# Stores of zeros issued twice, once more before the last part's loads of a decode-attention kernel

## The chip, the cores and the metric

The kernel runs on one core of a Trainium2 chip. The metric is device time in microseconds (us): the median of several runs of the whole program. Engines: TensorE (PE) does matmuls, VectorE (DVE), ScalarE (ACT) and GpSimd (POOL) do element work, and SyncE (SP) only issues transfers. Transfers run on 16 DMA engines; each engine of the core works through its own instructions in order.

## The reference

Two attention blocks decode one token and are mixed by a gate. Block A has 16 query heads with their own keys and values, block B 16 query heads on 8 key/value heads; each has 8192 cached positions of width 256, all in float32.

```python
def attend(x, k_cache, v_cache, wq, wo):                       # A: 16 kv heads, B: 8 (each serves two queries)
    q = (x @ wq).reshape(B, 1, 16, 256).transpose(0, 2, 1, 3)
    scores = jnp.einsum("bhqd,bhkd->bhqk", q, k) * (256 ** -0.5)
    o = jnp.einsum("bhqk,bhkd->bhqd", softmax(scores, axis=-1), v)
    return o.transpose(0, 2, 1, 3).reshape(B, 1, 16 * 256) @ wo

g = sigmoid((x * gate_w).sum(-1, keepdims=True))               # x: 1 x 1 x 448
out = g * attend(x, A...) + (1 - g) * attend(x, B...)          # 1 x 1 x 448
```

## The kernel before

All inputs but one weight lie in one array, `stream`, in the order of use. The kernel reads it once, front to back, through a ring of three large buffers, `slot_0` to `slot_2` (`SLOTS = 3`, each 128 partitions x 15872 floats, 8.1 MB). The list `LOADS`, made by `plan()`, has 54 entries; entry `number` fills the slot `number % 3`. Most entries are one transfer; the entry before last consists of three (the rest of one tile of values, and two whole tiles), and the last one, "the last part", of nine: the last tile of values in three pieces, three pieces of the output projection's weights, and three pieces of halves of the same weights. All these loads are issued by SP, on line 198 as every instruction that goes through the recorder.

The loop at the end of `build` sets the order of everything. For each entry it issues the entry's loads, and behind each load `piece` writes out the work on what it holds. Keys (`"k"`) become scores: for two of three heads on PE with a row of VectorE, ScalarE and VectorE work behind it (tiles `sc`, `mn`, `st`, `px`, `pr`), for the third, the heads `BY_ROW`, on VectorE, which multiplies the slot in place by the query (`slot<-slot,qa`) and reduces it (`sr<-slot`), 128 x 4096 numbers each time. Values (`"v"`) are multiplied by the weights `pr` on PE into `o`. When a head's keys are done, `gather` and `combine` (tiles `gs`, `mnr`, `ew`, `es`, `z`, `rz`, `wr`) make the softmax's sums; when its values are done, `take` copies `o` out (`px<-ps_o`, `ob`), `project_o` and `emit` apply the output weights. `wait` and `tick` put `combine` and `column` (tile `sel`) off by one or two tiles.

A recorder (`Recorder.call`) adds the semaphore waits: an instruction waits for what it depends on, through SBUF and PSUM, and on each engine the order is the order of the calls. A load into a slot waits until the work on the slot's earlier contents is done; a store waits until its source is written.

The result is one row of 448 numbers, held as four rows of 112 in the tile `ys`, and leaves in two stores, `store(0)` on ScalarE's queue and `store(1)` on SP's. At the end of the kernel each half is copied from PSUM into `ys` and stored. Before that the same two stores are issued once with zeros: `ys` is zeroed by VectorE among the constants, and the two stores stand in front of entry 3, the first that reuses a slot.

Of the kernel before, what the change touches and what calls it, by code (L numbers as in the profile page):

```python
# [28 lines left out]
SLOTS = 3  # L29
# [25 lines left out]
def plan():  # L55

    size = {"xg": XG, "k": ROWS * DH, "v": ROWS * DH, "wq": WQ, "wo": 8 * D}
    per = len(UNITS) * NT
    n = len(TILES)
    items = []  # L60
    for i in range(n + LEAD):
        if i == 0:
            items += [("xg", 0), ("wq", 0)]
        if i < n:
            items.append(("k", i))
        if i >= LEAD:
            items.append(("v", i - LEAD))
        if i % per == 7 and i // per + 1 < NS:
            items.append(("wq", i // per + 1))
        if i % per == LEAD + 1 and i >= per:  # L70
            items.append(("wo", i // per - 1))
    loads, room = [[]], FULL
    last = [("v", n - 3), ("v", n - 2)]
    for kind, i in items[:items.index(last[0])]:
        at, left = 0, size[kind]
        if (kind, i) == ("wq", DS):
            at, left = KF * 2 * DH, left - KF * 2 * DH
        while left:
            step = min(left, room) // ATOM[kind] * ATOM[kind]
            if step:  # L80
                loads[-1].append((kind, i, at, step))
            at, left, room = at + step, left - step, room - step
            if left:
                loads.append([])
                room = FULL

    loads = [[x] for x in loads]
    x = loads[-2][0]
    loads[-2] = [x[:2], x[2:]]
    loads[-1] += [[(kind, i, 0, size[kind])] for kind, i in last]  # L90
    at, end = 0, []
    for c in LAST_CUT:
        end.append([("v", n - 1, at, c * DH)])
        at += c * DH

    for h, n in ((0, 2), (1, 2), (3, 2)):
        end.append([("wo", NS - 1, 2 * h * D, n * D)])
    end += [[("half", 0, 0, D)], [("half", 1, 0, D // 2)], [("half", 1, D // 2, D // 2)]]
    return loads + [end]


LOADS = plan()
# [137 lines left out]
def program(nc, stream, dealt, out):  # L240
    nc.alloc_sbuf_tensor("pad", [P, -((nc.sbuf_base + 31) // 32 * 32) % 256 // 4 or 64], F32)
    memory = {("slot", i): nc.alloc_sbuf_tensor(f"slot_{i}", [P, FULL], F32) for i in range(SLOTS)}
    plan = Recorder(nc, memory)
    build(plan, stream, dealt, out)
    names = ["tensor", "vector", "scalar", "gpsimd"] + plan.dmas
    sems = {n: nc.alloc_semaphore(f"{n[0]}{n[1]}" if n[0] == "dma" else n) for n in names}
    rec = Recorder(nc, memory, plan.needed | {(e, plan.count[e] - 1) for e in names[:4]}, sems)
    stores = build(rec, stream, dealt, out)
    late = rec.wait("sync", [(e, rec.count[e] - 1) for e in names[:4]] + [d for d in rec.dmas if d not in stores[1:]])
    for sem, value in late:  # L250
        nc.sync.wait_ge(sem, value)
    nc.sync.sem_clear(range(sems[names[0]].num, sems[stores[1]].num))
    for d in stores[1:]:
        nc.sync.wait_ge(sems[d], 16)
    nc.sync.sem_clear(range(sems[stores[1]].num, sems[stores[-1]].num + 1))


def build(nc, stream, dealt, out):
# [323 lines left out]
        STORES.append(store(c))  # L582

    ys = const.tile([P, YN], F32, name="ys")
    nc.vector.memset(ys, 0.0)

    def store(c):

        to = out.rearrange("a b (g n) -> (a b g) n", g=NG)[2 * c:2 * c + 2, :]
        return (nc.scalar, nc.sync)[c].dma_start(to, ys[64 * c:64 * (c + 1)][::32, :])  # L590
# [67 lines left out]

    off = 0
    for number, fill in enumerate(LOADS):  # L660
        if number == SLOTS:
            store(0)
            store(1)
        buf = ring.tile([P, FULL], F32, name="slot")
        c = 0
        for load in fill:
            n = sum(x[3] for x in load)
            nc.sync.dma_start(buf[:, c:c + n], stream[off:off + P * n].rearrange("(p n) -> p n", p=P))
            off += P * n
            for x in load:  # L670
                piece(*x[:3], buf[:, c:c + x[3]])
                c += x[3]
# [79 lines left out]
```

## Time and profile before

| | |
|---|---|
| median of 3 runs | 1005.48 us (1005.34 to 1005.86) |
| profiled execution | 1005.52 us, span of its instructions 1004.2 us |
| PE busy | 584.8 us (58%) |
| DVE busy | 461.5 us (46%) |
| ACT busy | 94.1 us (9%) |
| POOL busy | 6.1 us (1%) |
| bytes moved by DMA | 432.49 MB, mean 431 GB/s |

The span runs from the first to the last instruction; the 1.3 us by which the execution is longer lie around it. Times in rows count from the span's start. A row of the profile's timeline gives start, length, engine, line, operation, output <- inputs, shapes and count, then in brackets how long the engine had been idle and what ended that. `SPq` and `ACTq` are the queues of SP and ScalarE as they issue transfers. The page's slices cut the span into 40 pieces of 25.1 us each.

### The profile page before, as it was taken

The numbers are of one execution on the slowest core, as the hardware profiler recorded it, in microseconds if no ns is written. First come the engines' busy times: TensorE is split into PE (matmuls) and PEld (weight loads), VectorE is DVE, ScalarE is ACT, GpSimd is POOL, SyncE is SP. The second block draws the span as 40 slices with busy tenths as digits, with TensorE's granted clock in tenths as the row PEclk, the third lists the DMA queues.
The fourth block names the chain that finished last, engine by engine and source line by source line (L and its number), as shares of the span: only waits on it lengthen the run. The fifth ranks groups of instructions, "written<-read, shape, count | busy, mean of one in ns | idle before, by whom it ended". The sixth has DMA issues, their size and how long they took to land.

```text
span 1004.2 us, 7432 instructions
## 1 busy us (share of the span) xinstructions
PE 584.8 (58%) x3162; PEld 171.7 (17%) x3162; DVE 461.5 (46%) x646; ACT 94.1 (9%) x308; POOL 6.1 (1%) x12
## 2 busy tenths in 40 slices
PE   1755755665753674646645565764655637636567
PEld 0211211121210221112111121111211112101112
DVE  3297222962249521486215851248521585215851
ACT  0100110001100110001100010100110000110011
POOL 2000000000000000000000000000000000000000
PEclk9877687678777887777777867777887777777888
DMA  9999999999999999999999999999999999999998
GB/s 395 442 438 432 426 436 444 422 433 438 443 428 422 441 443 427 420 445 438 428 430 438 435 428 440 430 431 435 433 443 422 431 443 433 431 427 443 435 414 363
DMA packets 9552, 432.49 MB, mean 431 GB/s; under 512 B 1145, under 2 KB 1529, under 8 KB 2169
## 3 DMA queue, kind: packets, MB, share of 16 engines
q1 hardware_dynamic: 9368, 431.24, 99.3%
q0 software_dynamic: 144, 0.79, 0.2%
q8 instruction: 24, 0.39, 0.1%
q14 instruction: 8, 0.07, 0.0%
q10 hardware_dynamic: 8, 0.00, 0.0%
HBM read 433.07 MB, written 0.00 MB: 431 GB/s over the span
## 4 chain that ended last, share of the span: by engine, by line
DMA 75%; PE 12%; DVE 12%; ACT 1%; issue 0%; SPq 0%; DVEq 0%
DMA slot<-in_stream_dram 75%; PE ps_o L198 6%; DVE sr L198 5%; DVE slot L198 5%; PE ps_sc L198 5%; PE ps_s L198 1%; DVE pr L198 1%; ACT px L198 1%; DVE mn L198 1%; ACT ew L198 0%; ACT pxr L198 0%; DVE st L198 0%; DVE wr L198 0%; PE ps_y L198 0%; DVE ob L198 0%
## 5 line engine op out<-in xcount | busy, mean ns | idle before, releaser
L198 PE MATMUL ps_o<-slot,pr 128*32 128x512 f32 (+1 forms) x1536 | 346.8, 759 | 227.9 <-DMA slot<-in_stream_dram 227.8
L198 PE MATMUL ps_sc<-slot,qb 128*32 128x512 f32 x1024 | 195.5, 734 | 98.0 <-DMA slot<-in_stream_dram 97.9
L198 DVE TENSOR_REDUCE mn<-ps_sc 128x1 f32<-128x512 f32 x64 | 44.1, 690 | 324.4 <-PE ps_sc L198 297.5
L198 DVE TENSOR_TENSOR slot<-slot,qa 128x4096 f32<-128x4096 f32 (+7 forms) x40 | 142.5, 3564 | 38.1 <-DMA slot<-in_stream_dram 38.1
L198 PEld LDWEIGHTS ps_o<-slot,pr 128*32 128x32 f32 (+1 forms) x1536 | 79.8, 142 | 408.7 <-DMA slot<-in_stream_dram 256.7
L198 DVE TENSOR_REDUCE sr<-slot 128x16 f32<-128x4096 f32 (+7 forms) x40 | 142.6, 3566 | 1.4
L198 PEld LDWEIGHTS ps_sc<-slot,qb 128*32 128x32 f32 x1024 | 46.2, 133 | 218.9 <-issue 116.0
L198 ACT ACTIVATE px<-ps_sc,st 128x512 f32<-128x512 f32 x64 | 44.0, 687 | 398.2 <-DVE st L198 398.2
L198 DVE STREAM_TRANSPOSE pr<-px 128x512 f32<-128x512 f32 x64 | 45.7, 714 | 54.1 <-ACT px L198 54.1
L198 PE MATMUL ps_s<-slot,xz 128*32 128x512 f32 (+1 forms) x130 | 41.5, 648 | 28.1 <-DVE xz L198 22.3
L198 ACT ACTIVATE pxr<-sr,st 128x16 f32<-128x16 f32 x32 | 9.8, 308 | 367.9 <-DVE st L198 367.9
L198 DVE SCALAR_TENSOR_TENSOR ob<-ps_o,half,px 128x256 f32<-128x256 f32 x24 | 11.3, 472 | 59.8 <-ACT px L198 59.6
L198 PE MATMUL ps_s<-sel,ob 128*128 128x1 f32 (+1 forms) x96 | 18.6, 298 | 33.9 <-DVE ob L198 33.9
L198 PEld LDWEIGHTS ps_s<-sel,ob 128*128 128x128 f32 x96 | 16.5, 242 | 57.9 <-DVE ob L198 48.7
L198 DVE TENSOR_TENSOR pr<-pxr,cols 128x256 f32<-128x256 f32 x32 | 13.6, 425 | 16.6 <-ACT pxr L198 16.6
L198 PEld LDWEIGHTS ps_s<-slot,xz 128*32 128x32 f32 (+1 forms) x130 | 10.4, 121 | 53.0 <-issue 24.0
L198 PE MATMUL ps_y<-slot,ocs 128*1 128x448 f32 (+1 forms) x176 | 16.4, 456 | 3.4 <-DMA slot<-in_stream_dram 3.2
L198 ACT ACTIVATE px<-ps_o,half 128x256 f32<-128x256 f32 x24 | 11.3, 470 | 58.5 <-PE ps_o L198 58.3
L198 PE MATMUL ps_s<-ones,wr 1*128 1x1 f32 x48 | 9.7, 270 | 11.2 <-DVE wr L198 11.1
L198 PE MATMUL ps_s<-px,rows 64*128 64x256 f32 x16 | 7.2, 539 | 13.1 <-DVE es L198 13.1
L198 PEld LDWEIGHTS ps_s<-ones,wr 1*128 1x128 f32 x48 | 7.7, 200 | 33.3 <-DVE wr L198 17.3
L198 ACT ACTIVATION_READ_ACCUMULATOR px<-ps_sc,st 128x1 f32 x64 | 12.3, 193 | 0.0
(69 smaller groups left out, 152.9 us busy)
## 6 DMA issues: line engine op xcount, KB each, us to landing
slot<-in_stream_dram SPq DMA_DIRECT2D x48, 7936.0 KB, 41.5
slot<-in_stream_dram SPq DMA_DIRECT2D x1, 7904.0 KB, 48.4
slot<-in_stream_dram SPq DMA_DIRECT2D x1, 7712.0 KB, 43.4
slot<-in_stream_dram SPq DMA_DIRECT2D x1, 7688.0 KB, 21.3
slot<-in_stream_dram SPq DMA_DIRECT2D x1, 5120.0 KB, 42.3
slot<-in_stream_dram SPq DMA_DIRECT2D x2, 2048.0 KB, 32.7
slot<-in_stream_dram SPq DMA_DIRECT2D x1, 2816.0 KB, 37.2
slot<-in_stream_dram SPq DMA_DIRECT2D x2, 1024.0 KB, 31.2
```

Source lines behind the costliest of these rows:

```text
L198: i = getattr(e, what)(*args, **kw)
```

## The change

The zeroing of `ys` is taken out of the constants. In front of entry 3, and a second time in front of the last part (entry 53), VectorE zeroes `ys` and the two stores are issued.

```diff
     ys = const.tile([P, YN], F32, name="ys")
-    nc.vector.memset(ys, 0.0)
...
     off = 0
     for number, fill in enumerate(LOADS):
-        if number == SLOTS:
+        if number in (SLOTS, len(LOADS) - 1):
+            nc.vector.memset(ys, 0.0)
             store(0)
             store(1)
         buf = ring.tile([P, FULL], F32, name="slot")
```

On VectorE the zeroing leaves its place before the first copy out of a load. In front of entry 3 it comes behind all that VectorE does with entries 0 to 2; `pr_2<-pxr_0,cols_0` ends the work on the last whole tile of keys in entry 2, `ob_0` is the first that needs entry 3. (The operation, the tiles with their buffer numbers, the shape, and what it waits for.)

```order
 L198 TENSOR_REDUCE st_1<-mt_0 128x1 [waits vector]
 L198 TENSOR_TENSOR pr_2<-pxr_0,cols_0 128x256 [waits scalar,tensor]
+L198 MEMSET ys_0 128x112
 L198 SCALAR_TENSOR_TENSOR ob_0<-ps_o_0,half_0,px_0 128x256 [waits scalar]
 L198 TENSOR_TENSOR slot_0<-slot_0,qa_0 128x4096
```

The memset is one instruction more between the two; nothing else moved there.

On SP, at the start of its list, rows of entries 2 to 7 and the store; the store's wait for VectorE is a wait for that memset.

```order
 L198 DMA slot_2<-in_stream_dram 128x15872
 L198 DMA out_0_dram<-ys_0 2x112 [waits vector]
-L198 DMA slot_0<-in_stream_dram 128x15872 [waits tensor]
-L198 DMA slot_1<-in_stream_dram 128x15872 [waits vector,tensor]
-L198 DMA slot_2<-in_stream_dram 128x15872 [waits vector,tensor]
+L198 DMA slot_0<-in_stream_dram 128x15872
+L198 DMA slot_1<-in_stream_dram 128x15872
+L198 DMA slot_2<-in_stream_dram 128x15872 [waits tensor]
 L198 DMA slot_0<-in_stream_dram 128x15872 [waits vector,tensor]
 L198 DMA slot_1<-in_stream_dram 128x15872 [waits tensor]
```

The order of SP's transfers is the same; the loads of entries 3 and 4 have no wait of their own any more, since the store's wait in front of them covers theirs.

On SP, at its end, the last two loads of the entry before last, then the last part:

```order
 L198 DMA slot_1<-in_stream_dram 128x4096 [waits tensor]
 L198 DMA slot_1<-in_stream_dram 128x4096 [waits vector]
-L198 DMA slot_2<-in_stream_dram 128x2048 [waits tensor]
-L198 DMA slot_2<-in_stream_dram 128x1024 [waits tensor] x2
-L198 DMA slot_2<-in_stream_dram 128x896 [waits tensor] x3
-L198 DMA slot_2<-in_stream_dram 128x448 [waits tensor]
+L198 DMA out_0_dram<-ys_0 2x112 [waits vector]
+L198 DMA slot_2<-in_stream_dram 128x2048
+L198 DMA slot_2<-in_stream_dram 128x1024 x2
+L198 DMA slot_2<-in_stream_dram 128x896 x3
+L198 DMA slot_2<-in_stream_dram 128x448
```

A store with a wait for VectorE now stands in front of the nine loads, which wait for nothing else. On VectorE, at the same place, the memset follows the end of `combine` for the last head:

```order
 L198 RECIPROCAL rz_1<-z_1 1x1 [waits vector]
 L198 TENSOR_SCALAR wr1_0<-ew_1,rz_1,gate_0 1x128 [waits vector]
+L198 MEMSET ys_0 128x112 [waits dma4,dma5]
 L198 SCALAR_TENSOR_TENSOR ob_1<-ps_o_2,half_0,px_1 128x256 [waits scalar]
-L198 COPY ys_0<-ps_y_0 64x112 [waits dma5,tensor]
+L198 COPY ys_0<-ps_y_0 64x112 [waits dma60,tensor]
```

The memset waits for the first pair of stores to be done with `ys`, and the final copies into `ys` wait for the second pair.

## The prediction

> **What bounds the kernel now.** I read the page first: the span, the slices, the DMA queues and the chain that ended last.
>
> ```profile
> span 1004.2 us, 7432 instructions
> DMA  9999999999999999999999999999999999999998
> GB/s 395 442 438 432 426 436 444 422 433 438 443 428 422 441 443 427 420 445 438 428 430 438 435 428 440 430 431 435 433 443 422 431 443 433 431 427 443 435 414 363
> q1 hardware_dynamic: 9368, 431.24, 99.3%
> q0 software_dynamic: 144, 0.79, 0.2%
> DMA 75%; PE 12%; DVE 12%; ACT 1%; issue 0%; SPq 0%; DVEq 0%
> ```
>
> The 16 DMA engines are busy in every slice, and queue 1, which carries the loads, takes 99.3% of their time. The best of 40 slices moves 445 GB/s, the mean is 431. So the kernel is one stream of 431 MB, and its time is that stream plus a short head and tail. Whatever empties the load queue costs its full length; work on the engines costs nothing as long as SyncE (SP) issues the next load before the queue runs dry. So the second question is how far ahead SP is. I take the first loads one by one: SP's issues, then the first instructions that waited for each load.
>
> ```profile
> 0.74 1.34 SPq L198 DMA_DIRECT2D slot<-in_stream_dram  x3
> 8.61 0.63 SPq L198 DMA_DIRECT2D out_dram<-ys  x1
> 37.14 0.33 SPq L198 DMA_DIRECT2D slot<-in_stream_dram  x1
> 59.46 0.33 SPq L198 DMA_DIRECT2D slot<-in_stream_dram  x1
> ...
> 22.12 0.40 DVE L198 COPY xz<-slot 128x3 f32<-128x3 f32 x3 [13.54 <-DMA slot<-in_stream_dram]
> 43.64 4.28 PE L198 MATMUL ps_sc<-slot,qb 128*32 128x512 f32 x18 [6.55 <-DMA slot<-in_stream_dram]
> 63.43 1.97 PE L198 MATMUL ps_o<-slot,pr 128*64 128x512 f32 x4 [8.99 <-DMA slot<-in_stream_dram]
> 82.12 3.68 PE L198 MATMUL ps_o<-slot,pr 128*64 128x512 f32 x6 [9.39 <-DMA slot<-in_stream_dram]
> 100.81 0.63 PE L198 MATMUL ps_sc<-slot,qb 128*32 128x512 f32 x3 [4.29 <-DMA slot<-in_stream_dram]
> ```
>
> Columns: start, duration, engine, operation; in brackets the idle time before and what ended it. Loads 0, 1 and 2 go out together at the start and land at 22.1, 43.6 and 63.4. Load 3 goes out at 37.14, as soon as PE has finished with slot 0, which is 26 us before load 2 lands, and itself lands at 82.1; load 4 at 100.8. A full load takes 18.7 us (82.12 to 100.81). SP runs about one and a half loads ahead, and that lead is the whole cover.
>
> **The change, part by part.** *The start.* The 0.15 us memset leaves VectorE's opening, which has idle time behind it (13.54 us before the first load lands): nothing. SP's store at 8.61 moves; it stood in front of a wait until 37.14: nothing gained.
>
> *The first pair of stores.* The memset now stands behind all that VectorE does with the first three loads, and SP's store and load 3 stand behind the memset. VectorE's rows from load 2 on:
>
> ```profile
> 63.41 4.42 DVE L198 TENSOR_TENSOR slot<-slot,qa 128x4096 f32<-128x4096 f32 x1 [0.33 <-DMA slot<-in_stream_dram]
> 67.87 4.42 DVE L198 TENSOR_REDUCE sr<-slot 128x16 f32<-128x4096 f32 x1
> ...
> 73.97 4.42 DVE L198 TENSOR_TENSOR slot<-slot,qa 128x4096 f32<-128x4096 f32 x1
> 78.42 4.42 DVE L198 TENSOR_REDUCE sr<-slot 128x16 f32<-128x4096 f32 x1
> ...
> 84.05 0.42 DVE L198 TENSOR_TENSOR pr<-pxr,cols 128x256 f32<-128x256 f32 x1 [0.54 <-ACT pxr L198]
> 86.35 0.48 DVE L198 SCALAR_TENSOR_TENSOR ob<-ps_o,half,px 128x256 f32<-128x256 f32 x1 [1.87 <-ACT px L198]
> L198 SPq DMA_DIRECT2D out_dram<-ys x2: 511/570/628, 8.6 to 1002.7; - x2
> L198 DVE MEMSET ys<- x1: 152/152/152, 8.4 to 8.4; 128x112 f32 x1
> ```
>
> The memset's predecessor in the new order is the row at 84.05; all before it needs only loads 0 to 2, so it keeps its time. The memset ends at 84.05 + 0.42 + 0.15 = 84.62. SP then issues its store, 0.63 us as the first one took, so load 3 goes out at about 85.3 instead of 37.14. Load 2 landed at 63.4: the queue is empty for over 20 us. What a load takes out of an empty queue is seen in the first one, and what a full one takes in the middle of the kernel beside it (size, median us from issue to landing):
>
> ```profile
> slot<-in_stream_dram SPq DMA_DIRECT2D x1, 7688.0 KB, 21.3
> slot<-in_stream_dram SPq DMA_DIRECT2D x48, 7936.0 KB, 41.5
> ```
>
> 21.3 us for 7688 KB; 248 KB more at 431 GB/s is 0.6, so 21.9. Load 3 lands at 85.3 + 21.9 = 107.2 instead of 82.1: 25.1 us late. From below: with 18.7 us for the load itself and 2 us for the empty queue (the first row less 18.3 us of its bytes at 431 GB/s leaves 3.0) it is 24. From above: after the kernel's own start, the second and third load took 21.5 and 19.8 us where 18.7 is the steady time, 3.9 in all; an indirect load of 0.79 MB, 1.8 us at 431 GB/s, lay in between, so up to 2.1 may belong to a queue that fills again, and the loss would be 27.2. I take 25.5, near the direct sum, since most of the early excess has that other owner. Nothing gives it back: loads 4 and 5 find their slots free and go out right behind load 3, but at the same rate.
>
> The Trainium skill ("DMA: Bandwidth & Descriptors", section "Anatomy of one DMA") fits a transfer, on GpSimd's path, as 2.0 us plus its bytes at 436 GB/s. An estimate by that page is 20.6 us for load 3, and the sum would be 1.3 us lower. The row of 21.3 us for the first load disagrees by the same 1.3 us, and it decides.
>
> ScalarE's store now waits for the same memset; behind it in ScalarE's order is the copy of ps_o (before the row at 86.35), which needs load 3 anyhow. No cost.
>
> *The second pair.* It stands before the last part's nine loads. SP today issues these long before they are needed; the rows are the last load of the part before (962.52), the first and the last of the nine, and then the work around the landing:
>
> ```profile
> 962.52 0.33 SPq L198 DMA_DIRECT2D slot<-in_stream_dram  x1
> 963.55 0.33 SPq L198 DMA_DIRECT2D slot<-in_stream_dram  x1
> 988.07 2.69 SPq L198 DMA_DIRECT2D slot<-in_stream_dram  x1
> 990.69 0.16 DVE L198 TENSOR_REDUCE mnr<-ps_s 1x1 f32<-1x16 f32 x1 [1.62 <-PE ps_s L198]
> 991.76 0.33 DVE L198 TENSOR_SCALAR wr<-ew,rz,gate 1x128 f32<-1x128 f32 x1
> 992.53 1.92 PE L198 MATMUL ps_o<-slot,pr 128*32 128x512 f32 x16 [1.89 <-DMA slot<-in_stream_dram]
> 1001.95 0.09 PEld L198 LDWEIGHTS ps_y<-slot,ocs 128*1 128x1 f32 x4 [0.20 <-DMA slot<-in_stream_dram]
> 1002.67 0.51 SPq L198 DMA_DIRECT2D out_dram<-ys  x1
> ```
>
> The load issued at 962.52 lands at 992.5 (PE waits for it). The memset comes behind wr, ending at 991.76 + 0.33 + 0.15 = 992.24; SP's store takes 0.5, so the nine loads start at about 992.8 on this clock, when the queue has just run dry. The nine hold 128 rows of 7680 floats together (2048, twice 1024, three times 896, 448, twice 224), 3.93 MB. At 431 GB/s that is 9.1 us, and with the 3.0 us of an empty queue the last lands at 1004.9, instead of 1001.9: +3.0. Issue does not limit: three issues took 1.34 us, nine take 4.0, under 9.1. From below: had the restart only 1 us, it is +1. From above: 990.69 waits for PE, and PE runs at half its granted clock for part of this stretch:
>
> ```profile
> 980.00:982.00 2.00, 1.65 (x8) 0.40 (x12) 0.00 (x0) 0.00 (x0) 0.00 (x0) 0.50 1.00 426
> 986.00:988.00 2.00, 2.00 (x24) 0.96 (x20) 0.85 (x2) 0.53 (x1) 0.00 (x0) 1.00 1.02 434
> 986.97 3.64 PE L198 MATMUL ps_o<-slot,pr 128*32 128x512 f32 x32
> ```
>
> The column before the last two is the granted clock: 0.50, then 1.00. If the half clock falls on the 3.64 us of matmuls at 986.97, memset and loads come 3.6 later, +6.6 in all. I take 2.6: the first of the nine holds 1 MB, so the engines that finish the old load early restart together, and the tail behind the last landing (1001.95 to the end) is unchanged.
>
> The second pair's own cover: ScalarE's store is issued after its copy of sel, which follows PE's work on the load that lands at 992.5, and is queued ahead of the copy of ps_o, which needs the late loads; the final writes of ys wait for both stores to land, some 8 us later. If a store from this place took over 8 us, that wait would show. The last stores are no faster: their 0.51 us is already below the 0.63 of the first.
>
> *The sum.* The profiled execution took 1005.52 us around its span of 1004.2, and the median of the runs is 1005.48, the same. 1005.52 + 25.5 + 2.6 = 1033.6 us, 2.8% slower.
>
> **The rivals.** *Only the first gap counts.* If the last part's loads start without a gap (because VectorE reaches the memset before the older load has landed, as it does by 0.3 us today), the time is 1005.5 + 24 to 25.5, about 1030.5. For it: 992.24 against 992.53. Against it: the queue must be refilled 3 us before it is dry.
>
> *The end gap is larger.* The half clock at the wrong place gives 1033.6 + 3.6 = 1037.2. For it: the clock alternates through the whole span, and a shift of 25 us changes where it falls. Against it: it stands at 1.00 from 986 to 1004 now.
>
> *The stores hold the queue.* The first store in SP's queue stood behind three loads, so no row shows one in front of a load on an idle queue. A write of 0.9 KB could block the engines it uses until it is received; its nearest price is the 0.7 us for which SP waits at the end for a store to land (below), twice, or at most some 2 us each: 1035 to 1037. The Trainium skill (same page, "Specifications") says that pieces under 512 B are read, modified and written; these rows have 448 B, and no row here shows what that costs.
>
> ```profile
> SPq L252 <- DMA out_dram<-ys: 0.7, 1, 0.7
> ```
>
> *Not slower: the stream wins it back.* If the 431 GB/s are set by consumers, not by the engines, three loads queued together could run faster afterwards. From 63.4 to 1001.9 the rest, 431.24 - 24.1 = 407.1 MB, moves in 938.5 us, 434 GB/s; to lose nothing it must move in 910.4, at 447. The best slice of the page has 445. It decides only if the whole stream runs above its best slice: 1005.5, within 0.2% (about 2 us, which is what can be told from no change here).
>
> **Chances.** Forecast 0.70 (1031.5 to 1036), only the first gap 0.10, larger end gap 0.10, stores holding the queue 0.07, not slower 0.03, split as 0.02 same and 0.01 faster. The range from 1030 to 1038 takes in the first four with the bounds 24 + 1 and most of 27.2 + 6.6; faster 0.01, same 0.02, slower 0.97.
>
> **What the profile would show.** Right: VectorE's memset of ys at about 84.5; SP's store there and three loads behind it, the first at about 85.3; some 22 us without DMA after 63; PE's wait for load 3 ending near 107; two digits of the DMA row low at the start; mean rate near 419 GB/s; a second memset behind the last wr and the nine issues in a row behind it, with 2 to 3 us of low DMA share. Wrong: load 3 issued before 80, or DMA at nine tenths in the second to fifth slice (then there is no gap), or the slices after it above 445 GB/s.

## The result, and the profile after

The changed kernel takes 1037.74 us (median of 6 runs, 1037.29 to 1039.19) against 1005.44: a ratio of 1.0323, 95% interval 1.0312 to 1.0334. It is 32 us slower; 1033.6 had been forecast, with a range up to 1038.0. The profiled execution took 1037.97 us around a span of 1035.5.

The page after the change: span, DMA slices and the queue of the loads.

```profile
span 1035.5 us, 7434 instructions
DMA  9926999999999999999999999999999999999997
GB/s 417 426 120 287 442 441 428 435 432 432 430 432 437 434 435 432 432 432 433 432 437 435 437 435 432 435 428 431 430 432 434 442 434 435 437 434 430 434 414 293
q1 hardware_dynamic: 9372, 431.24, 96.4%
```

The same bytes, and two low digits where there was none, in the third and fourth slices (a slice is 25.9 us here). Behind them the stream runs at its old rate up to the end, and no slice exceeds 442 GB/s. Around the first gap, the timeline of VectorE, SP and PE:

```profile
83.85 0.42 DVE L198 TENSOR_TENSOR pr<-pxr,cols 128x256 f32<-128x256 f32 x1 [0.54 <-ACT pxr L198]
84.25 0.15 DVE L198 MEMSET ys<- 128x112 f32 x1
84.42 0.63 SPq L198 DMA_DIRECT2D out_dram<-ys  x1
85.11 1.49 SPq L198 DMA_DIRECT2D slot<-in_stream_dram  x3
...
63.22 1.97 PE L198 MATMUL ps_o<-slot,pr 128*64 128x512 f32 x4 [8.80 <-DMA slot<-in_stream_dram]
106.77 3.67 PE L198 MATMUL ps_o<-slot,pr 128*64 128x512 f32 x6 [34.06 <-DMA slot<-in_stream_dram]
125.50 1.07 PE L198 MATMUL ps_sc<-slot,qb 128*32 128x512 f32 x3 [4.62 <-DMA slot<-in_stream_dram]
...
1008.88 3.64 PE L198 MATMUL ps_o<-slot,pr 128*32 128x512 f32 x16 [5.61 <-DMA slot<-in_stream_dram]
```

The memset ends at 84.40 (84.62 forecast), load 3 goes out at 85.1 (85.3) and lands at 106.77 (107.2) instead of 82.12: 24.7 us late. Load 4 is 24.7 late too (125.50 against 100.81). But one of the last loads is later still. In the kernel before it landed at 980.35:

```profile
980.35 3.64 PE L198 MATMUL ps_o<-slot,pr 128*32 128x512 f32 x16 [6.60 <-DMA slot<-in_stream_dram]
```

It now lands at 1008.88, 28.5 late. The lateness grew by 3.8 us between load 4 and this one, with the DMA row at nine tenths throughout; the forecast allowed for a loss of 27.2 us at most. The second gap, in the stretches around it (PE, PEld, DVE, ACT, POOL busy, granted clock, DMA share, GB/s) and on SP:

```profile
1016.00:1018.00 2.00, 2.00 (x24) 0.52 (x16) 0.79 (x2) 0.32 (x3) 0.00 (x0) 1.00 0.60 246
1018.00:1020.00 2.00, 0.65 (x10) 0.17 (x2) 0.87 (x5) 0.26 (x1) 0.00 (x0) 1.00 0.44 188
1020.00:1022.00 2.00, 0.97 (x12) 0.37 (x16) 0.22 (x2) 0.00 (x0) 0.00 (x0) 1.00 0.29 41
1022.00:1024.00 2.00, 1.26 (x14) 0.34 (x6) 0.00 (x0) 0.17 (x1) 0.00 (x0) 1.00 0.76 307
...
1020.07 0.15 DVE L198 MEMSET ys<- 128x112 f32 x1
1020.25 0.51 SPq L198 DMA_DIRECT2D out_dram<-ys  x1
1020.80 4.83 SPq L198 DMA_DIRECT2D slot<-in_stream_dram  x9
1021.03 1.92 PE L198 MATMUL ps_o<-slot,pr 128*32 128x512 f32 x16 [2.38 <-DMA slot<-in_stream_dram]
1033.74 0.50 SPq L198 DMA_DIRECT2D out_dram<-ys  x1
```

The DMA share falls from 1016 on, although the load in flight lands only at 1021.0: so some of the 16 engines have finished their part 3 to 4 us before others. The nine loads go out at 1020.8, 0.2 us before the slowest engine is done, and the last store at 1033.74 instead of 1002.67, 31.1 late: 2.6 more than before the gap. So the span's 31.3 us are 24.7 at the first gap, 3.8 that appear later, and 2.6 at the end with 0.2 behind the last store. The last 1.1 of the profiled execution's 32.4 us lie outside the span, where the runs of this kernel differ by as much (1.3 to 2.5 us).

### The profile page after: what moved, and what is told of

The parts are those of the page before. It is cut to its first block, busy times and chain, and to the rows that moved or that the text cites. A ratio compares the mean times of both kernels' runs of the same rounds, so it can differ in the third digit from the quotient of the medians.

```text
span 1035.5 us, 7434 instructions
## 1 busy us (share of the span) xinstructions
PE 592.4 (57%) x3162; PEld 174.5 (17%) x3162; DVE 461.8 (45%) x647; ACT 94.1 (9%) x308; POOL 6.1 (1%) x12
## 4 chain that ended last, share of the span: by engine, by line
DMA 70%; PE 15%; DVE 12%; ACT 1%; issue 1%; SPq 0%; another core or an unknown queue 0%; DVEq 0%
DMA slot<-in_stream_dram 70%; PE ps_o L198 7%; PE ps_sc L198 5%; DVE sr L198 5%; DVE slot L198 5%; PE ps_s L198 2%; DVE pr L198 1%; ACT px L198 1%; DVE mn L198 1%; ACT ew L198 0%; ACT pxr L198 0%; PE ps_y L198 0%; DVE wr L198 0%; DVE st L198 0%; SPq L198 0%
## 5 line engine op out<-in xcount | busy, mean ns | idle before, releaser
L198 PE MATMUL ps_o<-slot,pr 128*32 128x512 f32 (+1 forms) x1536 | 352.2, 766 | 252.1 <-DMA slot<-in_stream_dram 252.1
L198 PE MATMUL ps_s<-sel,ob 128*128 128x1 f32 (+1 forms) x96 | 18.7, 299 | 34.0 <-DVE ob L198 34.0
```

Source lines behind the costliest of these rows:

```text
L198: i = getattr(e, what)(*args, **kw)
```

## The experiments

Two theories for the 3.8 us. **Head start**: the DMA engines do not run in step; a load lands with its slowest engine, others are already at the next load, and an empty queue takes that lead from them. What a gap costs in the end is the standstill of the engines that were ahead. **Direct sum**: a gap costs what the next load is late, 24.7 us, and the rest belongs to the second pair.

**The first pair alone** (e1). The condition is `if number == SLOTS:`, with the memset in it.

> The first pair of stores alone waits behind VectorE's work on load 2; the second pair is left out. Theory 'head start': before the gap some DMA engines are several us ahead of others; the gap starts all of them together again, so load 3 is about 24.7 us late, and the lateness grows to about 28.5 us at the last loads: 1033.5 to 1034.5 us in all. Rival 'direct sum': lateness stays at 24.7 us after load 3, and what is missing of the 32 us belongs to the second pair: about 1030 us.

Measured 1034.6 us (1034.0 to 1035.54), ratio 1.029, interval 1.0273 to 1.0308.

```profile
107.44 3.62 PE L198 MATMUL ps_o<-slot,pr 128*64 128x512 f32 x6 [33.43 <-DMA slot<-in_stream_dram]
126.17 1.07 PE L198 MATMUL ps_sc<-slot,qb 128*32 128x512 f32 x3 [6.38 <-DMA slot<-in_stream_dram]
1009.27 3.24 PE L198 MATMUL ps_o<-slot,pr 128*32 128x512 f32 x16 [5.96 <-DMA slot<-in_stream_dram]
```

That is 25.3 and 25.4 late at loads 3 and 4, 28.9 at the load of 980.35: the growth belongs to the first gap. Direct sum's 1030 is out.

**The last pair alone** (e2).

```diff
-        if number == SLOTS:
+        if number == len(LOADS) - 1:
+            nc.vector.memset(ys, 0.0)
+        if number in (SLOTS, len(LOADS) - 1):
```

(The memset among the constants stays.)

> The first pair stands as before the change, the second pair with its memset stands in front of the last part's loads. Head start: the loads up to the one before the last part land as in the kernel before (992.5 us), the last part 1.5 to 3 us later, and the time is 1007 to 1009 us. Direct sum: the second pair carries all that the first does not, about 7 us: 1012 us. If the stores hold the queue, more than 3 us.

Measured 1008.38 us (1008.09 to 1010.0), ratio 1.003 (1.002 to 1.0041): 3.0 us. With the 29.2 us of e1 that is 32.2, the change's 32.3; the two gaps add up.

**The stores without the wait** (e3): as e2, but the second memset stands at `number == 40`.

> The first pair as before; the second pair in the same place in front of the last part's loads, but its memset stands thirteen entries earlier, so that SyncE and ScalarE find it long done: the stores without the wait. If only the wait costs: 1005.4 us, within 1 us. If a store in front of loads holds SyncE's queue: 1006.5 to 1009 us.

Measured 1005.43 us, ratio 1.0001 (0.9991 to 1.0011). A store in front of loads costs nothing that can be measured while the queue still has work: here it is issued some 29 us before the load in flight lands. On an empty queue no run has the loads without the store, but the changed kernel's load 3, behind its store, took 21.7 us (85.11 to 106.77), no more than the 21.9 that the kernel's first load, with no store in front, gives for its size.

**All stores of zeros on ScalarE** (e4): as changed, memsets included, with `store(0, nc.scalar)` and `store(1, nc.scalar)`.

> As changed, both memsets and both pairs where the change puts them, but all four stores of zeros are issued by ScalarE, so nothing of the change stands in SyncE's order. If SyncE's wait is the whole cost, load 3 goes out at 37 us again and the time is 1005.4 us, within 1 us. If memsets, VectorE's order or the stores themselves cost: up to 1008 us; if the cost is the whole of the change whoever issues, 1037 us.

Measured 1005.6 us, ratio 1.0 (0.9991 to 1.001). SP's first load behind the three again goes out when PE frees its slot:

```profile
36.89 0.33 SPq L198 DMA_DIRECT2D slot<-in_stream_dram  x1
82.14 3.67 PE L198 MATMUL ps_o<-slot,pr 128*64 128x512 f32 x6 [7.94 <-DMA slot<-in_stream_dram]
```

Memsets, VectorE's order and the number of stores are all free; the whole cost is that a store waits in SP's order in front of loads.

**Another deal of the early load** (e5, e6). An indirect load of 0.79 MB early in the kernel gives seven DMA engines 7 or 8 rows of 14 KB each and the other nine none. Here every engine gets 3 or 4, first in the kernel before, then with the first pair's gap.

```diff
-DEAL = {0: 8, 1: 7, 2: 8, 4: 8, 7: 8, 8: 8, 15: 8}
+DEAL = {g: 4 if g < 7 else 3 for g in range(16)}
```

> The kernel before with one table changed: the indirect load of 0.79 MB early in the kernel (some 14 KB a row, 55 rows) is dealt to all 16 DMA engines, 3 or 4 rows each, instead of 7 or 8 rows to seven of them. Head start: the seven engines with the extra load are the slow ones early, the other nine run 3 to 4 us ahead and use that up on the fetches of instructions later; dealt evenly the lead shrinks by some 2.4 us, so this is slower than the kernel before, 1006.5 to 1008 us. If the engines' leads do not matter: 1005.4 us.

Measured 1007.06 us, ratio 1.0015 (1.0005 to 1.0025). Loads 2 and 3 land earlier than in the kernel before, the late ones later:

```profile
61.72 1.98 PE L198 MATMUL ps_o<-slot,pr 128*64 128x512 f32 x4 [7.71 <-DMA slot<-in_stream_dram]
80.78 3.67 PE L198 MATMUL ps_o<-slot,pr 128*64 128x512 f32 x6 [8.68 <-DMA slot<-in_stream_dram]
981.84 3.64 PE L198 MATMUL ps_o<-slot,pr 128*32 128x512 f32 x16 [5.62 <-DMA slot<-in_stream_dram]
```

1.7 and 1.3 us early, 1.5 late at the end. By the head start, the lead that the uneven deal gives nine engines is worth that much over the kernel.

> The evenly dealt load together with the first pair of stores alone. Head start: load 2 lands some 2 us earlier than with the uneven load, the wait for VectorE starts and ends earlier, and after the gap all engines start together whatever the deal: 1031.5 to 1033.5 us, below the 1034.6 of the first pair alone, though the even deal by itself costs time. If the engines' leads do not matter: 1034.6 us or, should the even deal cost something by itself, that more.

Measured 1033.29 us (1032.98 to 1034.03), ratio 1.0275 (1.0258 to 1.0292). By the medians the same gap costs 26.2 us where the deal is even and 29.2 where it is uneven, so the two edits don't add up. The rows of e6:

```profile
105.48 3.68 PE L198 MATMUL ps_o<-slot,pr 128*64 128x512 f32 x6 [33.81 <-DMA slot<-in_stream_dram]
1007.58 3.64 PE L198 MATMUL ps_o<-slot,pr 128*32 128x512 f32 x16 [6.76 <-DMA slot<-in_stream_dram]
```

Against the same loads of e5, 80.78 and 981.84, that is 24.7 us late at load 3 and 25.7 at the end. With the even deal the lateness grows by 1.0 us, with the uneven one by 3.6 (e1). The stretch before the gap shows why; first e6, then the changed kernel:

```profile
55.00:60.00 5.00, 0.00 (x0) 0.00 (x0) 4.36 (x5) 0.40 (x2) 0.00 (x0) 0.65 0.94 406
60.00:62.00 2.00, 0.27 (x2) 0.27 (x4) 1.23 (x7) 0.53 (x2) 0.00 (x0) 0.50 0.01 4
```
```profile
55.00:60.00 5.00, 0.00 (x0) 0.00 (x0) 4.90 (x4) 0.00 (x0) 0.00 (x0) 0.71 0.76 330
60.00:62.00 2.00, 0.00 (x0) 0.00 (x0) 0.80 (x5) 0.93 (x4) 0.00 (x0) 0.50 0.31 131
62.00:64.00 2.00, 0.78 (x2) 0.29 (x4) 1.65 (x5) 0.00 (x0) 0.00 (x0) 0.50 0.00 0
64.00:85.00 21.00, 8.71 (x32) 2.57 (x28) 19.05 (x14) 0.80 (x4) 0.00 (x0) 0.74 0.00 0
```

Dealt evenly, the engines run dry nearly together (0.94, then 0.01). Dealt unevenly they do so over several us (0.76, 0.31). From 55 to 86 that is 1.2 + 1.4 + 24 = 26.6 us of standstill for the mean engine, so less for the slowest and more for those ahead, though the profile does not tell the engines apart; the end is 28.5 us late.

**The memset one entry earlier** (e7): the first pair alone, its memset at `number == SLOTS - 1`, the stores where they were.

> The first pair alone, with its memset one entry earlier in VectorE's order: behind the work on loads 0 and 1, ahead of that on load 2. SyncE then issues its store and load 3 at about 64 us instead of 84, when load 2 has landed by 0.5 us. Head start: the slow engines stand still for about 3 us, the ones ahead for about 6.5, so load 3 comes 3 to 4 us late and the total is 1010.5 to 1013 us. Direct sum: 1008 to 1009.5 us. If only waits much longer than a load count: 1005.4 us.

Measured 1012.73 us (1012.51 to 1013.96), ratio 1.0072 (1.0055 to 1.0089): as the head start had it, above direct sum's 1009.5.

```profile
63.52 0.63 SPq L198 DMA_DIRECT2D out_dram<-ys  x1
85.66 3.36 PE L198 MATMUL ps_o<-slot,pr 128*64 128x512 f32 x6 [12.53 <-DMA slot<-in_stream_dram]
987.75 3.64 PE L198 MATMUL ps_o<-slot,pr 128*32 128x512 f32 x16 [6.32 <-DMA slot<-in_stream_dram]
```

Load 3 goes out 21 us earlier than in the changed kernel and the cost falls by about as much (7.2 us against 29.2 in e1). It is 3.5 us late at load 3 and 7.4 at the end: even where the gap lasts about 3 us, about 4 more appear later.

**The same gap later in the kernel** (e9, e10): the second memset and pair at `number == 23` or `number == 43` instead of the last part.

> The kernel before with the second memset and pair of stores not in front of the last part but in front of entry 23, behind VectorE's work on entry 22, which like that on entry 2 lasts some 21 us after its load has landed. Head start: load 23 comes about 24 us late, as load 3 did, but by 440 us a part of the engines' lead has been used up, so the lateness grows by only 1 to 2.5 us until the end: 1030.5 to 1032.5 us. If every restart costs the same 3.6 us later, wherever it is: 1033.5 us. Direct sum: 1029.5 us.

> The same in front of entry 43, behind VectorE's work on entry 42, again 21 us after its load has landed. Head start: load 43 comes about 24 us late and, the lead being nearly used up at 812 us, the lateness grows by less than 1 us: 1029.3 to 1030.5 us. If every restart costs the same: 1033.5 us.

Measured 1032.65 us (1031.87 to 1033.47), ratio 1.0271 (1.0253 to 1.0288), and 1031.45 us (1031.06 to 1031.63), ratio 1.0256 (1.0239 to 1.0273). Both lie above what was expected, by 0.15 and 1.0 us: the load right behind the gap is 24.4 and 24.9 us late where 24 was expected, and about 1 us more appears at the second. The first two loads behind the gap and the late load, first for entry 23, then for entry 43; then rows of the kernel before:

```profile
480.89 3.38 PE L198 MATMUL ps_o<-slot,pr 128*32 128x512 f32 x16 [23.87 <-DMA slot<-in_stream_dram]
500.74 2.77 PE L198 MATMUL ps_o<-slot,pr 128*32 128x512 f32 x10 [4.83 <-DMA slot<-in_stream_dram]
1006.88 3.21 PE L198 MATMUL ps_o<-slot,pr 128*32 128x512 f32 x16 [6.06 <-DMA slot<-in_stream_dram]
```
```profile
855.53 3.41 PE L198 MATMUL ps_o<-slot,pr 128*32 128x512 f32 x16 [25.45 <-DMA slot<-in_stream_dram]
875.22 2.77 PE L198 MATMUL ps_o<-slot,pr 128*32 128x512 f32 x9 [4.67 <-DMA slot<-in_stream_dram]
1006.15 3.64 PE L198 MATMUL ps_o<-slot,pr 128*32 128x512 f32 x16 [6.08 <-DMA slot<-in_stream_dram]
```
```profile
437.75 9.52 PE L198 MATMUL ps_o<-slot,pr 128*64 128x512 f32 x32 [5.85 <-DMA slot<-in_stream_dram]
475.15 2.78 PE L198 MATMUL ps_o<-slot,pr 128*32 128x512 f32 x10 [2.76 <-DMA slot<-in_stream_dram]
830.60 3.64 PE L198 MATMUL ps_o<-slot,pr 128*32 128x512 f32 x16 [0.46 <-DMA slot<-in_stream_dram]
849.31 2.77 PE L198 MATMUL ps_o<-slot,pr 128*32 128x512 f32 x9 [3.70 <-DMA slot<-in_stream_dram]
```

PE did not wait for load 23 in the kernel before, so its landing there is put at 437.75, where load 22 landed, plus the 18.7 us of a load.

| gap in front of entry | first load behind it, late by | second, late by | load of 980.35, late by | growth from the first | growth from the second |
|---|---|---|---|---|---|
| 3 (e1) | 25.3 | 25.4 | 28.9 | 3.6 | 3.6 |
| 23 (e9) | 24.4 | 25.6 | 26.5 | 2.1 | 0.9 |
| 43 (e10) | 24.9 | 25.9 | 25.8 | 0.9 | -0.1 |

The later the gap, the less appears afterwards, from whichever load it is counted, as it must if the lead is used up over the kernel. A fixed price of a restart would have given the same growth in each row. (In e1 1.1 of the 3.6 us appear by the load that landed at 157.0 before and lands at 183.46 there, so about 1 us comes early in every row.)

**The last pair with an earlier memset** (e11): as e2, the memset at `number == len(LOADS) - 2`.

> The last pair alone, in the same place of SyncE's order, with its memset one entry earlier in VectorE's order: in front of the sums of the last head (mnr, es, z, wr) and behind gs, which ended at 989.1 us in the kernel before. The nine loads then go out at about 989.7 us instead of 992.35, some 2.5 us before the queue's slowest engine is dry. Head start: the cost falls from 3.0 us to between 0 and 1 us: 1005.4 to 1006.4 us. If the cost of the last pair is in the stores or the final copies that wait for them, it stays: 1008.4 us.

Measured 1005.84 us (1005.35 to 1007.47), ratio 1.0005 (0.9996 to 1.0014): no measurable cost, from 3.0 us.

```profile
988.05 0.15 DVE L198 MEMSET ys<- 128x112 f32 x1
988.80 4.72 SPq L198 DMA_DIRECT2D slot<-in_stream_dram  x9
992.32 1.92 PE L198 MATMUL ps_o<-slot,pr 128*32 128x512 f32 x16 [2.67 <-DMA slot<-in_stream_dram]
```

The nine loads go out 3.5 us before the load in flight lands; 0.2 us before was not enough.

**No stores of zeros** (e8): the kernel before without the first pair.

> The kernel before without any stores of zeros. If they prepare the queues for the final stores: the first issue of a store on ScalarE's queue takes 1.1 us instead of 0.5 at the end, and the time is 1005.8 to 1006.5 us. If they do nothing: 1005.4 us, within 0.5 us.

Measured 1005.97 us, ratio 1.0004 (0.9994 to 1.0014): no difference that can be told. The profile shows what was expected of the single issue: ScalarE's store at the end takes 1.09 us, where it took 0.51 in the kernel before. None of these kernels beats the one before.

## Why the prediction was right, and where it was off

- **The direction and the mechanism** were right: e4 puts the whole cost on SP's wait, and e3 finds no cost in a store that does not wait.
- **The step up to load 3** was right to 0.5 us, issue and landing alike. The Trainium skill ("DMA: Bandwidth & Descriptors", "Anatomy of one DMA") would give, estimated by its fit for GpSimd's path, 20.6 us for this load, which SP issues. It took 21.7 (85.11 to 106.77), so the measurement decides here too.
- **The term of the first gap was mis-sized**: 25.5 forecast, 28.5 measured at the last loads (29.2 in the total of e1). The failing step is "I take 25.5, near the direct sum". It priced the gap by the landing of the next load, and that is set by the slowest of the engines. The excess seen at the kernel's start (21.5 and 19.8 us for the second and third load) was put down to the indirect load as a thing of the past. In part it came from that load's uneven deal (1.7 us of it goes with the even deal, e5), which leaves nine engines ahead; the gap takes their lead. The upper bound of 27.2 was therefore too low.
- **The term of the second gap** held: 2.6 forecast, 2.6 in the span, 3.0 in e2. The match is in part luck: the forecast had the queue run dry all at once where the old load lands, and in the trace the DMA share falls from 1016, 5 us before the landing. Its lower rival, "only the first gap counts", is out by e2.
- **The half clock** did fall into the tail (0.51 to 0.63 from 1026 to 1030), but not where the rival had put it: the matmuls ahead of the memset ran at 1.00.
- **Stores that hold the queue**: not seen (e3, and load 3 behind its store). **The stream wins it back**: not seen; the slices behind the gap are at 428 to 442 GB/s up to the last two, below the 447 that it needed.
- The total lies inside the range but above the forecast's own 1036. The profiled execution is 4.4 us above the sum: 3.0 are the excess of the first term, 1.1 lie outside the span, and 0.2 behind the last store. That the range holds it is luck: its upper end made room for the half clock ahead of the memset, which did not come.

What uses the lead up can be read from the packets in the traces, though no run takes it away. From 100 us on, 18 loads in the thirteen traces land 19.3 to 19.9 us behind the load before them, where 18.7 is the rule. Between the two landings there is each time one fetch of instructions (queue q8, a packet of 16 KB that takes 0.88 to 0.97 us), while of all 560 such pairs of landings only 266 have one. All 18 stand behind a gap or in e5, where the even deal gives no lead; the other kernels have the same 24 or 25 fetches and no such step. Behind the gap there are three of them in e1 (landings at 145.75, 446.62 and 784.34), two in e9 (500.74 and 819.72) and one in e10 (875.22), which is most of the growth in the table. The early 1 us in e7, whose load 5 is 4.6 us late after 3.5 at load 4, has its fetch too, at 108.2.

What is not shown: on which of the 16 engines a fetch runs, and so that it is the lead of that engine which hides it in the kernel before; and why many fetches behind a gap leave no step. No run moves or removes a fetch.

## What to carry to other kernels

A wait placed in the order of the engine that issues loads stalls every load behind it, whatever it is for: look up what the awaited instruction itself stands behind, and compare its time with the moment at which the queue runs dry. Stores whose source is ready late belong on another queue (e4), or their source should be made ready before the queue begins to run dry: an entry earlier was enough at the end (e11), but still cost 7.2 us at the start (e7). A gap in a stream that is the bound is to be priced by the engines that are ahead, not by the one that ends the load; the DMA share just before a queue runs dry shows how far apart they are.

## What the hardware showed unexpectedly

The landings say that the 16 DMA engines keep a lead over each other for hundreds of us: 0.79 MB dealt unevenly at 28 to 51 us is still felt at 980 (1.7 us earlier at load 2 and 1.5 later at the end, when dealt evenly), and an empty queue takes most of it away (growth of 3.6 us in e1, 1.0 in e6). That a load lands with its last engine agrees with the Trainium skill ("DMA: Bandwidth & Descriptors", "Why a DMA increments its semaphore by 16 and not by 1"), by which the engines of one transfer finish independently and only the full count means that all has landed; here the DMA share was 0.44 from 1018 to 1020 with that landing at 1021.0.
